# Weights' signs restored by ScalarE's rectifier, VectorE's sign step, floor and low-bit steps removed

## The chip, the cores and the metric

The kernel runs on one NeuronCore of a Trainium2 chip. The metric is the device time of one execution in microseconds (us), taken as the median of several runs. TensorE (PE in the profile, PEld for its weight loads) does the matrix products, VectorE (DVE), ScalarE (ACT) and GpSimd (POOL) the elementwise work, and SyncE (SP) issues the transfers. Each engine runs its own instructions in the order in which they were written into its queue; engines meet only where one waits for another.

## The reference, cut to what matters

Attention with a threshold on 4 batches of 8 heads (576 positions, 64 wide) gives 2304 tokens of width 512. Two dense layers follow, each an expansion to 2048 and a contraction back to 512.

```python
thresh = np.max(scores, axis=-1, keepdims=True) - tau
scores = np.where(scores >= thresh, scores, -1000000000.0)
...
h = x @ w_in
sp = np.where(h > 20.0, h, np.log1p(np.exp(np.minimum(h, 20.0))))
g = h * np.tanh(sp)
return (g @ w_out).astype(np.float32)
...
h = x @ w_in
relu6 = np.clip(h + 3.0, 0.0, 6.0)
g = h * relu6 / 6.0
return (g @ w_out).astype(np.float32)
```

The four weight matrices come in as 64-bit floats.

## The kernel before, in words

The program is written by a planner: a list of tasks, each with the engines that may run it, a cost and a priority, is turned once into a fixed order of instructions for every engine. A table of nudges (`NUDGE`) and the costs set this order; no order is found at run time.

In time it falls into three stages. Up to about 405 us the attention runs tile by tile: scores (`s_s`, L1849) on TensorE, row maximum (`nm_pk`, L1858) and mask (`e_ex`, L1871) on VectorE, exponential on ScalarE, the low half of the split into two 16-bit floats on GpSimd (`p_ph`, L729), a transposing transfer (`pt_tr`, L1884) and the product with the values (`aux_pv`, L1897). The scores tiles lie in two banks of PSUM, and the mask is what frees a bank. The expansion of the first dense layer (`h_g`, L1241) is threaded between these. From about 405 to 640 us comes the contraction of the first dense layer (`y_y`, L1356): ScalarE applies the activation Mish to a stored tile (`hp_e`, L1327) and makes the high half (`gs_h`, L1330), VectorE the low half (`gs_h`, L1336). After 640 us the second dense layer runs.

The weights of all four matrices (m = 0 to 3) are converted on the side, 8 groups of 128 x 1024 words each, 32 conversions. The 64-bit words are loaded (`raw_lr`, L881). VectorE takes the largest magnitude of the high halves (`top`, L785), from which a power of two as scale follows in a few steps on single columns (`group_scale`; L796, L799 to L810). For m = 0 and 2 the maximum is first spread over the partitions: a diagonal (`dgb_zd`, L756, on ScalarE) is multiplied on TensorE (L761) and reduced on VectorE (L764). Then `one_conversion` makes 32-bit floats: ScalarE multiplies the high half with the scale (c1, L921, into the tile `cvt`), VectorE or GpSimd shifts it left by three bits (c2, L931 or L929), VectorE copies the sign bit from the raw word (c3, L937) and then inserts bits of the low half (c4, L942). Two 16-bit halves are made of it (`w__h`, `w__u`). c1 of m = 0 and 1 lies in the attention stage; c1 of m = 2 and 3, 16 conversions, lies between 431 and 624 us, between the instructions of the first layer's contraction. The same diagonals serve to scale the layers' inputs and outputs (`dgb_zdy`).

Of the kernel before, what the change touches and what calls it, by code (L numbers as in the profile page):

```python
# [8 lines left out]
F32 = mybir.dt.float32  # L9
# [6 lines left out]
AF = mybir.ActivationFunctionType  # L16
ALU = mybir.AluOpType
# [23 lines left out]
ORDER_OUT = (0, 5, 6, 4, 2, 3, 1)  # L41
INF_BITS = 0x7F800000
TINY = 2.0 ** -100
FLOOR = 2.0 ** -13
WARM_WINDOW = 3.413
RELEASE = dict.fromkeys(("s", "m", "h", "y", "aux"), 0.27)

# [51 lines left out]
JOIN_FROM = 340.468  # L99
STAY = 0.954  # L100
NBLK_EARLY = 2 * B - 2
NUDGE = {
# [407 lines left out]
class Plan:  # L510
# [19 lines left out]
    def add(  # L530
        self, engines, fn, deps=(), bufs=(), prio=None, off=0.0, dma=0.0, name="", order=()
    ):
        shift = NUDGE.get(name, 0.0)
        prio, off = (None, off + shift) if prio is None else (prio + shift, off)
# [149 lines left out]
def fused_kernel(ctx: ExitStack, tc, q, k, v, tau, w1i, w1o, w2i, w2o, out):  # L684
    nc = tc.nc
# [42 lines left out]
    def sub(e, dst, a, b):  # L728
        engine[e].tensor_tensor(dst, a, b, ALU.subtract)  # L729

    def pick(which, **cost):
        return {e: cost[e] for e in WHO[which]}
# [14 lines left out]
    def bits(t):  # L747
        return t.bitcast(U32)

    def spread(task, name, src, held, ring, after):  # L750

        dg, pm = Buf(r_dgb), Buf(ring)

        def diag(e):
            if e == "act":
                nc.scalar.activation(dg.tile, ident, AF.Copy, scale=src())  # L756
            else:
                nc.vector.tensor_scalar_mul(dg.tile, ident, src())

        def total(e):  # L760
            mm(pm.tile[:, :P], ones, dg.tile, start=True, stop=True)  # L761

        def top(e):
            nc.vector.tensor_reduce(src(), pm.tile[:, :P], AX.X, ALU.max)  # L764

        a = task({"dve": 0.3, "act": 0.4}, diag, [after], [*held, dg], "zd" + name)
        a = task({"pe": 0.06}, total, [a], [dg, pm], "zp" + name)
        return task({"dve": 0.28}, top, [a], [*held, pm], "zt" + name)
# [4 lines left out]
    wt, r_w, converted, scaled_by, wsc = {}, {}, {}, {}, {}  # L773

    def high(raw):
        return bits(raw.tile).rearrange("p a (n t) -> p a n t", t=2)[:, :, :, 1]
# [14 lines left out]
    def group_scale(task, name, m, i, ring, after):  # L791

        top, sc, inv = (wsc[m][k][:, i : i + 1] for k in ("top", "sc", "is"))

        def cut(e):
            nc.vector.tensor_scalar(bits(top), bits(top), 0x7FFF0000, None, ALU.bitwise_and)  # L796

        def factor(e):
            nc.vector.tensor_scalar(top, top, FLOOR, None, ALU.max)  # L799
            nc.vector.tensor_scalar(  # L800
                bits(sc), bits(top), INF_BITS, INF_BITS, ALU.bitwise_and, ALU.bitwise_xor
            )
            if m == 0:
                nc.vector.tensor_scalar_mul(inv, sc, 2.0 ** -111)
            nc.vector.tensor_scalar_mul(sc, sc, 2.0 ** -112)
            if m == 0:
                nc.vector.tensor_scalar(
                    bits(inv), bits(inv), 3, INF_BITS, ALU.logical_shift_left, ALU.bitwise_and
                )
                nc.vector.tensor_scalar(bits(inv), bits(inv), INF_BITS, None, ALU.bitwise_xor)  # L810

        a = after
        if m % 2 == 0:
            a = task({"dve": 0.15}, cut, [a], [], "za" + name)
            a = spread(task, name, lambda: top, [], ring, a)
        return task({"dve": 0.97 if m == 0 else 0.5}, factor, [a], [], "zf" + name)

# [55 lines left out]
    def tasker(at):  # L873
        def task(engines, fn, deps, bufs, tag, dma=0.0):
            return add(engines, fn, deps, bufs, at, 0.0 if at is not None else MOE_OFF, dma, tag)

        return task
# [7 lines left out]
    def convert(m, src, pool, prio, off, ring):  # L885
# [23 lines left out]
            scaled_parts[:] = [factors[i : i + step] for i in range(0, NG, step)]  # L909
        scaled_by[m] = summary(tasker(prio + 2 * NG * off), m, ring, factors)  # L910

    def one_conversion(m, g, raw, deps, task):
        nm = f"{m}_{g}_"
        t = Buf(r_cvt)
        dst = wt[m][g]

        def low():
            return bits(raw.tile).rearrange("p a (n t) -> p a n t", t=2)[:, :, :, 0]

        def c1(e):  # L920
            nc.scalar.activation(  # L921
                t.tile.bitcast(F32), high(raw).bitcast(F32), AF.Copy,
                scale=wsc[m]["sc"][:, g : g + 1],
            )

        def c2(e, j):
            if e == "pool":
                ti = t.tile[:, j].bitcast(I32)
                nc.gpsimd.tensor_tensor(ti, ti, eight.to_broadcast([P, DM]), ALU.mult)  # L929
                return  # L930
            nc.vector.tensor_scalar(  # L931
                t.tile[:, j], t.tile[:, j], 3, 0x7FFFFFF8, ALU.logical_shift_left,
                ALU.bitwise_and,
            )

        def c3(e):
            nc.vector.scalar_tensor_tensor(  # L937
                t.tile, high(raw), 0x80000000, t.tile, ALU.bitwise_and, ALU.bitwise_or
            )

        def c4(e):
            nc.vector.scalar_tensor_tensor(  # L942
                t.tile, low(), 29, t.tile, ALU.logical_shift_right, ALU.bitwise_or
            )

        a = task(EXPAND, c1, deps, [raw, t], "c" + nm)
        b = [
            task(
                pick(f"c{m}{j}", **SHIFT) if m > 1 else SHIFT, lambda e, j=j: c2(e, j), [a], [t],
                f"c{nm}{j}",  # L950
            )
            for j in range(2)
        ]
        a = task({"dve": 1.28}, c3, b, [raw, t], "c" + nm)
        a = task({"dve": 1.28}, c4, [a], [raw, t], "c" + nm)
        if m > 1:
            combined(m, g, t, a, task)
            return

        def hi(e):  # L960
            nc.scalar.activation(dst.tile[:, :, 0], t.tile.bitcast(F32), AF.Copy)

        def lo(e, j):
            sub(e, dst.tile[:, j, 1], t.tile[:, j].bitcast(F32), dst.tile[:, j, 0])

        a = task({"act": 1.05}, hi, [a], [t, dst], "h" + nm)
        for j in range(2):
            converted[m, 2 * g + j] = task(
                {"pool": 1.25, "dve": 0.68}, lambda e, j=j: lo(e, j), [a], [t, dst], f"u{nm}{j}"
            )  # L970
# [289 lines left out]
    def inner(blk, early, at=None, gap=0.0):  # L1260

        task = planner(at, gap, f"0_{blk}")
        if blk == 2 * B:
            x, src = Buf(r_x), Buf(r_sum)

            def tails_of():
                return src.tile

            def get(e):
                nc.sync.dma_start(out=tails_of(), in_=td)  # L1270

            a = task({"sp": 0.5}, get, tails, [src], "xt", 1.46)
            ready = [
                split(task, f"0_{blk}", src, tails_of, x, xinv[:, B:], r_h, [a])
            ]
            input_scales(B, ready[0], None if at is None else at)
        else:
            x, ready = x_of.pop(blk)
        hscale, scaled = hin[:, blk // 2], hin_done[blk // 2]
        for fp in range(NG):  # L1280
            h = Buf(r_h)
            last = gemm1(task, 0, fp, PIECE if early else 12, x, h, ready)
            if fp % 2 == 0:
# [780 lines left out]
    t = 0  # L2064
# [3 lines left out]
    for b in range(B):  # L2068
        units = [(hp, cs) for cs in halves for hp in range(NPAIR)]
        tiles = {}  # L2070
        for i, (hp, cs) in enumerate(units):
# [4 lines left out]
            t = tiles[hp](t, cs)  # L2076
# [68 lines left out]
    task = tasker(at)  # L2145
# [81 lines left out]
```

## Time and profile before

| what | value |
|---|---|
| median of 3 runs | 985.71 us (985.18 to 986.22) |
| profiled execution | 984.73 us, its span 982.9 us |
| TensorE busy | 922.2 us (94%) |
| VectorE busy | 797.9 us (81%) |
| ScalarE busy | 650.8 us (66%) |
| GpSimd busy | 409.2 us (42%) |

The span is the time from the first to the last instruction in the profile; the 1.8 us beside it lie around it. Busy shares are means over stages that differ, so the stages have to be read one by one.

### The profile page before, as it was taken

How to read it: one execution, taken by the hardware profiler on the slowest of the kernel's cores; microseconds unless marked ns; L12 is line 12 of the kernel's file. 1: busy time of each engine (PE TensorE's matmuls, PEld its weight loads, DVE VectorE, ACT ScalarE, POOL GpSimd, SP SyncE). 2: the span in 40 equal slices, each digit the busy share in tenths (PEclk: the TensorE clock that was granted, in tenths of full speed). 3: DMA queues.
4: the chain of work that ended last, by engine and by line, in shares of the span. 5: the costliest groups of instructions: out<-in, count | busy, mean ns of one | idle time of the engine just before them, and what ended most of it. 6: DMA issues, size and time to landing. Idle time of an engine off the chain costs nothing.

```text
span 982.9 us, 25896 instructions
## 1 busy us (share of the span) xinstructions
PE 922.2 (94%) x10776; PEld 797.2 (81%) x10776; DVE 797.9 (81%) x1516; ACT 650.8 (66%) x1051; POOL 409.2 (42%) x354
## 2 busy tenths in 40 slices
PE   3669779999999999999999999999999999999996
PEld 1447457777777778888888888899999999999986
DVE  6998898888878888569999889888758758758864
ACT  6678688888888877567866778655444444545541
POOL 2777776766655667315656777720000000000000
PEclk9769789999999999999999999999999999999999
DMA  9899999999999999864654757750110110110001
GB/s 313 179 233 234 228 226 218 251 253 217 238 217 270 216 220 238 234 239 173 239 211 176 282 188 287 246 219 9 60 47 16 60 41 22 60 32 31 23 15 31
DMA packets 201798, 164.48 MB, mean 167 GB/s; under 512 B 174160, under 2 KB 174928, under 8 KB 195280
## 3 DMA queue, kind: packets, MB, share of 16 engines
q1 hardware_dynamic: 201680, 162.82, 61.1%
q8 instruction: 85, 1.39, 0.6%
q14 instruction: 33, 0.27, 0.1%
HBM read 84.28 MB, written 36.04 MB: 122 GB/s over the span
## 4 chain that ended last, share of the span: by engine, by line
PE 76%; DVE 13%; POOL 3%; DMA 3%; issue 2%; ACT 1%; SPq 0%; DVEq 0%; POOLq 0%; ACTq 0%
PE h_g L1241 15%; PE y_y L1356 13%; PE s_s L1849 7%; PE aux_pv L1897 5%; PE hp_g1a L1430 5%; PE h_g0a L1430 5%; PE hp_g1d L1430 2%; PE h_g0d L1430 2%; DMA pt_tr<-p_ph 2%; DVE e_ex L1871 2%; DVE nm_pk L1858 1%; POOL p_ph L729 1%; DVE top L785 1%; PE h_g1b L1430 1%; DVE gs_h L1336 1%
## 5 line engine op out<-in xcount | busy, mean ns | idle before, releaser
L729 POOL TENSOR_TENSOR p_ph<-e_ex,p_ph 128x128 f16<-128x128 f32 (+3 forms) x160 | 192.5, 1225 | 106.4 <-issue 54.8
L1583 PEld LDWEIGHTS <-gs_h 128*128 128x128 f16 x1512 | 146.8, 98 | 18.0 <-issue 1.5
L1430 PEld LDWEIGHTS <-w__h 128*128 128x128 f16 x2016 | 156.0, 98 | 1.2 <-issue 0.6
L1871 DVE SCALAR_TENSOR_TENSOR e_ex<-s_s,thr_th,e_ex 128x576 f32<-128x576 f32 x144 | 111.9, 812 | 15.3 <-ACT thr_th L1863 11.8
L1858 DVE TENSOR_REDUCE nm_pk<-s_s 128x1 f32<-128x576 f32 x144 | 104.6, 751 | 18.0 <-PE s_s L1849 17.0
L1868 ACT ACTIVATE e_ex<-s_s,nm_pk 128x576 f32<-128x576 f32 x144 | 104.1, 730 | 18.5 <-DVE nm_pk L1858 13.9
L1849 PE MATMUL s_s<-kd_lk,qs_qp 64*128 64x288 f32 x440 | 80.8, 480 | 36.4 <-DVE e_ex L1871 25.6
L1876 ACT ACTIVATE p_ph<-e_ex 128x576 f16<-128x576 f32 x144 | 94.8, 678 | 13.5 <-DVE e_ex L1871 9.1
L1430 PEld LDWEIGHTS <-w__u 128*128 128x128 f16 x1008 | 98.6, 98 | 0.0
L1897 PEld LDWEIGHTS <-pt_tr 128*128 128x128 f16 x2016 | 81.3, 103 | 11.1 <-issue 5.8
L1849 PEld LDWEIGHTS s_s<-kd_lk,qs_qp 64*128 64x128 f32 x440 | 41.4, 204 | 59.0 <-issue 39.5
L1897 PE MATMUL aux_pv<-vh,pt_tr 128*128 128x65 f16 (+1 forms) x1296 | 86.1, 203 | 1.9 <-DMA pt_tr<-p_ph 1.9
L729 DVE TENSOR_TENSOR gs_h<-g_ab,gs_h 128x896 f16<-128x896 f32 x72 | 74.6, 1087 | 15.9 <-ACT gs_h L1533 15.9
L1533 ACT ACTIVATE gs_h<-g_ab 128x1792 f16<-128x1792 f32 x36 | 59.6, 1690 | 27.4 <-DVE g_ab L729 27.4
L1897 PE MATMUL aux_pv<-vl_vl,pt_tr 128*128 128x64 f16 x720 | 70.7, 203 | 0.0
L1517 ACT ACTIVATE g_ab<-g_ab,aux,hscales 128x512 f32<-128x512 f32 x72 | 54.1, 804 | 16.9 <-DVE g_ab L1458 16.9
L1327 ACT ACTIVATE hp_e<-hl_l 128x512 f32<-128x512 f32 x72 | 42.4, 594 | 23.5 <-DVE gs_h L1336 23.2
L1290 ACT ACTIVATE he_t<-h_g,hin 128x512 f32<-128x512 f32 x63 | 42.9, 683 | 19.0 <-PE h_g L1241 15.1
L1523 DVE SCALAR_TENSOR_TENSOR g_ab<-g_ab,f 128x512 f32<-128x512 f32 x72 | 51.2, 747 | 5.0 <-ACT g_ab L1517 5.0
L1336 DVE SCALAR_TENSOR_TENSOR gs_h<-hp_e,fscales,gs_h 128x512 f16<-128x512 f32 x72 | 53.0, 743 | 2.1 <-ACT gs_h L1330 2.1
L1330 ACT ACTIVATE gs_h<-hp_e,fscales 128x512 f16<-128x512 f32 x72 | 47.3, 678 | 7.6 <-PE y_y L1356 6.8
L1448 ACT ACTIVATE s_ka<-h_g0a 128x512 f32<-128x512 f32 x27 | 16.1, 595 | 48.1 <-PE h_g0a L1430 47.9
(672 smaller groups left out, 2559.2 us busy)
## 6 DMA issues: line engine op xcount, KB each, us to landing
hd<-he_t SPq DMA_DIRECT2D x36, 512.0 KB, 4.2
hl_l<-hd SPq DMA_DIRECT2D x18, 1024.0 KB, 5.7
raw_lr<-in_moe_w_in SPq DMA_DIRECT2D x16, 1024.0 KB, 6.0
raw_lr<-in_moe_w_out SPq DMA_DIRECT2D x16, 1024.0 KB, 7.5
yd<-yl_zhy SPq DMA_DIRECT2D x9, 896.0 KB, 3.8
qs_qp<-in_q SPq DMA_DIRECT2D x10, 576.0 KB, 5.8
v_lv<-in_v SPq DMA_DIRECT2D x16, 320.0 KB, 4.7
kd_lk<-in_k SPq DMA_DIRECT2D x15, 288.0 KB, 3.9
```

The costliest lines, as they stand in the source:

```text
L729: engine[e].tensor_tensor(dst, a, b, ALU.subtract)
L1241: mm(hv[:, j, :], wj[:, wl, c * P : (c + 1) * P], x.tile[:, c, xl, :], start=j == 0 and n == 0, stop=j == 1 and n == 11, skip_group_check= ...
L1336: nc.vector.scalar_tensor_tensor(s.tile[:, k, 1], g.tile.rearrange("p (a n) -> p a n", a=2), fs[:, fp : fp + 1], s.tile[:, k, 0], ALU.mult ...
L1356: mm(yv[:, h, :], wt[1][f // 2].tile[:, f % 2, wl, c * P : (c + 1) * P], gs[fp // COL].tile[:, fp % COL, gl, f % 2, :], start=fp == 0 and ...
L1430: mm(dst.tile[:, i * Q : (i + 1) * Q], wt[2][fp][wl].tile[:, right - 1, c * P : (c + 1) * P], x[xl].tile[:, c, left - 1], start=first and ...
L1583: mm(region(p), part[:, gl, left - 1], wt[3][fp][wl].tile[:, right - 1], start=fp == n == 0 and spot(p)[1] == 0, stop=fp == NG - 1 and n == 2,
L1849: mm(s[j].tile[:, half, :HALF], lh[r], rh[r], start=m == 0, stop=m == len(terms) - 1,)
L1858: nc.vector.tensor_reduce(neg.tile[:, j : j + 1], sv(j), AX.XY, ALU.max, negate=True)
L1868: nc.scalar.activation(ev(j), sv(j), AF.Exp, bias=neg.tile[:, j : j + 1])
L1871: nc.vector.scalar_tensor_tensor(ev(j), sv(j), thr.tile[:, j : j + 1], ev(j), ALU.is_ge, ALU.mult)
L1876: nc.scalar.activation(p16.tile[:, js, :S], e_.tile[:, js], AF.Copy)
L1897: mm(ov[:, dst, :d], pt.tile[:, j, ch, :], part.tile[:, src, vc, :], start=i == j == ch == 0 and part is vh, stop=j == w - 1 and ch == 8, ...
```

## The change

c1 becomes a rectifier (`AF.Prelu`) whose slope for negative inputs is minus 2 to the 32nd: a negative word comes out positive, with the exponent bit of weight 32 set. The shift by three moves that bit into the place of the sign, and the mask of the shift keeps it. So VectorE's sign step c3 falls away, in all 32 conversions. The maximum is no longer cut to its upper bits (16 instructions, m = 0 and 2) and no longer floored (32 instructions); instead the scale is bounded in the multiplication that was there. The tasks stay in the planner with their costs, as empty functions.

```diff
-        def cut(e):
-            nc.vector.tensor_scalar(bits(top), bits(top), 0x7FFF0000, None, ALU.bitwise_and)
-
         def factor(e):
-            nc.vector.tensor_scalar(top, top, FLOOR, None, ALU.max)
-            nc.vector.tensor_scalar(
-                bits(sc), bits(top), INF_BITS, INF_BITS, ALU.bitwise_and, ALU.bitwise_xor
-            )
+            ts = nc.vector.tensor_scalar
+            ts(bits(sc), bits(top), INF_BITS, INF_BITS, ALU.bitwise_and, ALU.bitwise_xor)
             if m == 0:
-                nc.vector.tensor_scalar_mul(inv, sc, 2.0 ** -111)
-            nc.vector.tensor_scalar_mul(sc, sc, 2.0 ** -112)
+                ts(inv, sc, 2.0 ** -111, 2.0 * CAP, ALU.mult, ALU.min)
+            ts(sc, sc, 2.0 ** -112, CAP, ALU.mult, ALU.min)
...
+    def idle(e):
+        pass
...
             nc.scalar.activation(
-                t.tile.bitcast(F32), high(raw).bitcast(F32), AF.Copy,
-                scale=wsc[m]["sc"][:, g : g + 1],
+                t.tile.bitcast(F32), high(raw).bitcast(F32), AF.Prelu,
+                scale=wsc[m]["sc"][:, g : g + 1], alpha=NEGATIVE,
             )
...
-                t.tile[:, j], t.tile[:, j], 3, 0x7FFFFFF8, ALU.logical_shift_left,
+                t.tile[:, j], t.tile[:, j], 3, 0xFFFFFFF8, ALU.logical_shift_left,
...
-        def c3(e):
-            nc.vector.scalar_tensor_tensor(
-                t.tile, high(raw), 0x80000000, t.tile, ALU.bitwise_and, ALU.bitwise_or
-            )
...
-        a = task({"dve": 1.28}, c3, b, [raw, t], "c" + nm)
+        a = task({"dve": 1.28}, idle, b, [raw, t], "c" + nm)
```

The order of the remaining instructions is unchanged on every engine; TensorE, GpSimd and SyncE have the same rows as before. Line numbers behind the change are 8 lower for most of the code. VectorE has 1373 rows in place of 1454.

VectorE during the first conversion (m = 0, group 0), before: the spread maximum, the sign step of `cvt_c_0`, the floor (L799) and the scale of the next group, then the attention.

```order
L764 TENSOR_REDUCE top_146<-aux_zp_1_1_414 128x1
L1967 TENSOR_SCALAR den_dt_0_2_430<-aux_pv_0_0_1_306 128x4
L937 SCALAR_TENSOR_TENSOR cvt_c_0__1_377<-raw_lr_0_0_199,cvt_c_0__1_377 128x1024
L1970 RECIPROCAL den_dt_0_2_430<-den_dt_0_2_430 128x4
L799 TENSOR_SCALAR top_146<-top_146 128x1
L800 TENSOR_SCALAR sc_147<-top_146 128x1
L804 TENSOR_SCALAR is_149<-sc_147 128x1
L805 TENSOR_SCALAR sc_147<-sc_147 128x1
L807 TENSOR_SCALAR is_149<-is_149 128x1
L810 TENSOR_SCALAR is_149<-is_149 128x1
L1974 TENSOR_TENSOR xn_dn_0_2_445<-aux_pv_0_0_1_306,den_dt_0_2_430 128x256
L1858 TENSOR_REDUCE nm_pk_1_0_1_448<-s_s_1_0_0_425 128x1
```

The same place now:

```order
L765 TENSOR_REDUCE top_146<-aux_zp_1_1_411 128x1
L1959 TENSOR_SCALAR den_dt_0_2_427<-aux_pv_0_0_1_305 128x4
L1962 RECIPROCAL den_dt_0_2_427<-den_dt_0_2_427 128x4
L798 TENSOR_SCALAR sc_147<-top_146 128x1
L800 TENSOR_SCALAR is_149<-sc_147 128x1
L801 TENSOR_SCALAR sc_147<-sc_147 128x1
L803 TENSOR_SCALAR is_149<-is_149 128x1
L804 TENSOR_SCALAR is_149<-is_149 128x1
L1966 TENSOR_TENSOR xn_dn_0_2_440<-aux_pv_0_0_1_305,den_dt_0_2_427 128x256
L1850 TENSOR_REDUCE nm_pk_1_0_1_443<-s_s_1_0_0_422 128x1
```

The sign step and the floor are gone; what stood behind them moves up.

ScalarE has 977 rows in place of 945. The 32 new ones are loads of activation tables (`ACT_TABLE_LOAD`), put in when the program is built: one ahead of each rectifier of m = 2 and 3, and one ahead of the next Mish. There are none at the 16 conversions of the attention stage, and the two loads that stood in the program before stand there still. ScalarE at the conversion of group 4 of m = 2 (c1 is `cvt_c_4`), before:

```order
L1330 ACTIVATE gs_h_0_2_1_7513<-hp_e_0_2_1_7588,fscales 128x512
L921 ACTIVATE cvt_c_4__1_7632<-raw_lr_4_0_7407,sc_6626 128x1024
L1327 ACTIVATE hp_e_0_3_1_7649<-hl_l_0_3_0_7480 128x512
L1290 ACTIVATE he_t_0_8_1_7515<-h_g_0_0_8_1_7498,hin 128x512
L1327 ACTIVATE hp_e_0_3_1_7657<-hl_l_0_3_0_7480 128x512
L997 ACTIVATE w__h_3_0_2_7607<-sum_q_3_0_1_7605 128x1024
L1111 ACTIVATE xf_zvy_1_0_1_1_7686<-y_y_0_0_1_0_7162,sm_zmy_1_0_1_1_7534 128x512 x2
L1330 ACTIVATE gs_h_0_3_1_7705<-hp_e_0_3_1_7649,fscales 128x512
L1330 ACTIVATE gs_h_0_3_1_7705<-hp_e_0_3_1_7657,fscales 128x512
L756 ACTIVATE dgb_zd_5_0_7723<-ident,top_6625 128x128
```

The same place now:

```order
L1322 ACTIVATE gs_h_0_2_1_7461<-hp_e_0_2_1_7535,fscales 128x512
L918 ACT_TABLE_LOAD
L918 ACTIVATE cvt_c_4__1_7578<-raw_lr_4_0_7356,sc_6586 128x1024
L1319 ACT_TABLE_LOAD
L1319 ACTIVATE hp_e_0_3_1_7595<-hl_l_0_3_0_7429 128x512
L1282 ACTIVATE he_t_0_8_1_7463<-h_g_0_0_8_1_7446,hin 128x512
L1319 ACTIVATE hp_e_0_3_1_7603<-hl_l_0_3_0_7429 128x512
L989 ACTIVATE w__h_3_0_2_7554<-sum_q_3_0_1_7552 128x1024
L1103 ACTIVATE xf_zvy_1_0_1_1_7632<-y_y_0_0_1_0_7116,sm_zmy_1_0_1_1_7481 128x512 x2
L1322 ACTIVATE gs_h_0_3_1_7650<-hp_e_0_3_1_7595,fscales 128x512
L1322 ACTIVATE gs_h_0_3_1_7650<-hp_e_0_3_1_7603,fscales 128x512
L757 ACTIVATE dgb_zd_5_0_7667<-ident,top_6585 128x128
```

Two table loads stand around the rectifier; nothing else moved.

## Rows read from the trace of the kernel before

**Rows 1.** The page: the span, and TensorE's busy time, share and instructions.
```profile
span 982.9 us, 25896 instructions
...
PE 922.2 (94%) x10776; PEld 797.2 (81%) x10776; DVE 797.9 (81%) x1516; ACT 650.8 (66%) x1051; POOL 409.2 (42%) x354
```

**Rows 2.** Windows by stage: length; PE, PEld, DVE, ACT, POOL busy (count); PEclk; DMA.
```profile
25.00:80.00 55.00, 36.63 (x391) 26.39 (x389) 52.85 (x109) 38.85 (x67) 41.40 (x36) 0.72 0.85 198
...
98.00:140.00 42.00, 29.32 (x282) 19.90 (x278) 36.12 (x77) 30.92 (x57) 28.66 (x28) 0.80 1.03 233
...
140.00:200.00 60.00, 60.00 (x748) 47.55 (x749) 54.27 (x102) 50.89 (x93) 44.40 (x39) 1.00 1.03 231
...
460.00:530.00 70.00, 67.83 (x624) 60.46 (x622) 68.10 (x118) 50.62 (x75) 41.79 (x30) 1.00 0.50 177
...
530.00:640.00 110.00, 109.99 (x1019) 98.66 (x1019) 95.83 (x163) 82.60 (x121) 83.01 (x61) 1.00 0.70 254
```

**Rows 3.** TensorE's longest waits, 25 to 80 us, then 98 to 140 us: total, times, longest.
```profile
PE s_s L1849 <- DVE e_ex L1871: 12.3, 7, 4.1
...
PE s_s L1849 <- DVE e_ex L1871: 7.6, 3, 3.5
```

**Rows 4.** Timeline, GpSimd then VectorE: start, length, instruction, [idle before, releaser].
```profile
66.78 2.26 POOL L729 TENSOR_TENSOR w__h__1_806<-cvt_c__1_694,w__h__1_806 128x512 f16<-128x512 f32 x2 [4.58 <-ACT w__h__1_806 L961]
...
111.29 1.43 DVE L937 SCALAR_TENSOR_TENSOR cvt_c__1_1405<-raw_lr,cvt_c__1_1405 128x1024 uint32<-128x1024 uint32 x1 [1.67 <-POOL cvt_c__1_1405 L929]
...
114.88 1.22 DVE L785 TENSOR_REDUCE top<-raw_lr 128x1 f32<-128x1024 f32 x1 [1.49 <-DMA raw_lr<-in_moe_w_in]
```

**Rows 5.** Windows, line L937 (the sign step) alone: VectorE busy (count), PEclk, DMA.
```profile
25.00:80.00 55.00, 5.67 (x4) 0.72 0.85 198
...
98.00:140.00 42.00, 3.93 (x3) 0.80 1.03 233
```

**Rows 6.** VectorE's lines: the floor, with its count, busy us and mean ns.
```profile
L799 DVE TENSOR_SCALAR top<-top 128x1 f32<-128x1 f32 x32 | 4.6, 145 | 0.1
```

**Rows 7.** ScalarE's timeline around the one table load in its midst.
```profile
413.10 0.69 ACT L1290 ACTIVATE he_t<-h_g,hin 128x512 f32<-128x512 f32 x1 [1.98 <-PE h_g L1241]
413.81 1.28 ACT L1327 ACT_TABLE_LOAD   x1
415.10 1.12 ACT L1327 ACTIVATE hp_e<-hl_l 128x512 f32<-128x512 f32 x2
```

**Rows 8.** ScalarE's timeline at three conversions, and a diagonal for TensorE.
```profile
455.95 1.24 ACT L921 ACTIVATE cvt_c__1_7295<-raw_lr,sc 128x1024 f32<-128x1024 f32 x1 [2.05 <-DVE sc L805]
...
463.32 1.25 ACT L921 ACTIVATE cvt_c__1_7392<-raw_lr,sc 128x1024 f32<-128x1024 f32 x1 [1.56 <-DVE sc L805]
...
475.07 0.60 ACT L1327 ACTIVATE hp_e<-hl_l 128x512 f32<-128x512 f32 x1 [2.71 <-DVE gs_h L1336]
...
480.26 1.24 ACT L921 ACTIVATE cvt_c__1_7632<-raw_lr,sc 128x1024 f32<-128x1024 f32 x1
481.38 0.59 ACT L1327 ACTIVATE hp_e<-hl_l 128x512 f32<-128x512 f32 x1
...
486.42 0.40 ACT L756 ACTIVATE dgb_zd<-ident,top 128x128 bf16<-128x128 f32 x1
```

**Rows 9.** TensorE's timeline: a spread matmul and its one stall at 530 us.
```profile
488.23 0.22 PE L761 MATMUL h_zp<-dgb_zd,ones 128*128 128x128 bf16 x1
...
530.01 1.47 PE L1241 MATMUL h_g<-x_zh,w__h__1_1766 128*128 128x256 f16 x12 [2.10 <-DVE he_t L1292]
```

**Rows 10.** Windows, line L921 (c1) alone: ScalarE busy (count), PEclk, DMA.
```profile
460.00:530.00 70.00, 7.44 (x6) 1.00 0.50 177
530.00:640.00 110.00, 8.64 (x7) 1.00 0.70 254
```

**Rows 11.** ScalarE's waits for VectorE and for TensorE, 530 to 640 us.
```profile
ACT hp_e L1327 <- DVE gs_h L1336: 9.5, 12, 1.5
ACT gs_h L1330 <- PE y_y L1356: 6.3, 4, 2.6
```

More of the change, by code (lines that the diff above doesn't have):

```diff
@@ L43 @@
 TINY = 2.0 ** -100
-FLOOR = 2.0 ** -13
+CAP = 2.0 ** -98
 WARM_WINDOW = 3.413
@@ L101 @@
 NBLK_EARLY = 2 * B - 2
+NEGATIVE = -(2.0 ** 32)
 NUDGE = {
@@ L793, in group_scale @@
         top, sc, inv = (wsc[m][k][:, i : i + 1] for k in ("top", "sc", "is"))
-        def cut(e):
-            nc.vector.tensor_scalar(bits(top), bits(top), 0x7FFF0000, None, ALU.bitwise_and)
         def factor(e):
-            nc.vector.tensor_scalar(top, top, FLOOR, None, ALU.max)
-            nc.vector.tensor_scalar(
-                bits(sc), bits(top), INF_BITS, INF_BITS, ALU.bitwise_and, ALU.bitwise_xor
-            )
+            ts = nc.vector.tensor_scalar
+            ts(bits(sc), bits(top), INF_BITS, INF_BITS, ALU.bitwise_and, ALU.bitwise_xor)
             if m == 0:
-                nc.vector.tensor_scalar_mul(inv, sc, 2.0 ** -111)
-            nc.vector.tensor_scalar_mul(sc, sc, 2.0 ** -112)
+                ts(inv, sc, 2.0 ** -111, 2.0 * CAP, ALU.mult, ALU.min)
+            ts(sc, sc, 2.0 ** -112, CAP, ALU.mult, ALU.min)
             if m == 0:
-                nc.vector.tensor_scalar(
-                    bits(inv), bits(inv), 3, INF_BITS, ALU.logical_shift_left, ALU.bitwise_and
-                )
-                nc.vector.tensor_scalar(bits(inv), bits(inv), INF_BITS, None, ALU.bitwise_xor)
+                ts(bits(inv), bits(inv), 3, INF_BITS, ALU.logical_shift_left, ALU.bitwise_and)
+                ts(bits(inv), bits(inv), INF_BITS, None, ALU.bitwise_xor)
         a = after
         if m % 2 == 0:
-            a = task({"dve": 0.15}, cut, [a], [], "za" + name)
+            a = task({"dve": 0.15}, idle, [a], [], "za" + name)
             a = spread(task, name, lambda: top, [], ring, a)
@@ L931, in c2 @@
             nc.vector.tensor_scalar(
-                t.tile[:, j], t.tile[:, j], 3, 0x7FFFFFF8, ALU.logical_shift_left,
+                t.tile[:, j], t.tile[:, j], 3, 0xFFFFFFF8, ALU.logical_shift_left,
                 ALU.bitwise_and,
-            )
-        def c3(e):
-            nc.vector.scalar_tensor_tensor(
-                t.tile, high(raw), 0x80000000, t.tile, ALU.bitwise_and, ALU.bitwise_or
             )
```

## Prediction

> **What bounds the kernel now.** I read the page first, then windows cut by stage, then TensorE's waits in the stages where it is not full, then ScalarE's and VectorE's timelines where the change touches them. TensorE is busy 922.2 us of the span of 982.9 us [rows 1]; what can be won without less matrix work is in the other 60 us. The windows say where they lie. From 25 to 80 us TensorE is busy 36.63 of 55 us and from 98 to 140 us 29.32 of 42 us, while VectorE is busy 52.85 and 36.12; from 140 us on TensorE is full, and from 530 to 640 us it is busy 109.99 of 110 us [rows 2]. In the first two stages it waits above all for the mask that frees a scores bank, 12.3 and 7.6 us [rows 3]. So there VectorE sets the pace, helped by a granted clock of 0.72 and 0.80, that is 1.2 GHz for part of the time [rows 2]. Behind that TensorE sets the end: an engine that works off its queue in order, and is full, keeps any head start that it gets, and passes on any wait that it is given. The change therefore has two terms: what VectorE gives TensorE before 140 us, and what the new table loads cost it between 455 and 640 us.
>
> **Term one: VectorE before 140 us.** In 25 to 80 us four sign steps take 5.67 us, in 98 to 140 us three take 3.93 us [rows 5]. The floor takes 145 ns [rows 6] and stands there eight times (once a conversion, all of m = 0), 1.2 us; the low-bit step, one column like it, stands there six times, by the same row 0.9 us. Together 5.67 + 3.93 + 1.2 + 0.9 = 11.7 us. That is the upper bound. The lower is 0: if GpSimd, the transfers or ScalarE held the pace, VectorE would only idle more. GpSimd is busy 41.40 of 55 us, and its chain shows up in the critical path, but its long waits are for halves that ScalarE can make only once VectorE has finished the word: 4.58 us at 66.78 us [rows 4], so it moves up with VectorE. One step gives nothing: that at 111.29 us waited 1.67 us for GpSimd and took 1.43 us, and shortly behind it VectorE waits 1.49 us for a load of raw words [rows 4]; without the step it would wait there instead. That leaves 10.3 us. Instructions overlap by about a tenth of a microsecond, and here and there the mask will find its exponential not ready. I take 7 us, nearer the upper end because VectorE idles only 2 us of 55 in the first stage. The other 25 sign steps buy TensorE nothing directly, since it is full where they stand: its own matrix work hides them, and if it ran out, each would be worth its 1.2 to 1.4 us again.
>
> The rectifier itself costs what the copy did, as far as rows go: c1 takes 1.24 to 1.25 us [rows 8] on the same 1024 columns, and no row shows a rectifier. I take 0, with a bound of one overlap, 0.1 us, an instruction.
>
> **Term two: 32 table loads on ScalarE.** The load in the middle of the program takes 1.28 us; the copy ahead of it runs from 413.10 for 0.69 us and so ends at 413.79, the load begins at 413.81 and the Mish behind it at 415.10 [rows 7]. So the load stands in the open and costs 1.31 us. Elsewhere neighbours overlap: the c1 at 480.26 lasts 1.24 us, yet the Mish behind it begins at 481.38, 0.12 us before c1 ends [rows 8]. A load between the two takes this away as well: about 1.41 us a load, 45 us in all.
>
> The Trainium skill's page "ScalarE: Activation LUTs", section "What ACT_TABLE_LOAD costs", gives about 1283 ns for the load, as the row has it, and on top of it some 1380 ns of drain, 2.66 us a switch. The trace shows no such drain around its load [rows 7]; by the page 32 loads would cost 85 us, and the sum would come out near the second rival's, below. The same page, section "Table sets: the hidden batching unit", says to group calls by table set and not to alternate, which speaks against this order.
>
> From 460 to 530 us ScalarE is busy 50.62 of 70 us, from 530 to 640 us 82.60 of 110 us [rows 2]. Six conversions fall into the first window and seven into the second [rows 10], two loads each: 12 and 14 loads, 16.9 and 19.7 us. That makes 67.5 of 70 and 102.3 of 110. The loads fit, but only just. Most of ScalarE's idle time there is waiting for VectorE, which the change unloads, and a load stands ahead of the wait of its successor, so it can run inside it: 2.05 us at 455.95, 1.56 at 463.32, 2.71 at 475.07 [rows 8]; between 530 and 640 us such waits are 9.5 us, and 6.3 us more are for TensorE to free a tile [rows 11], which means that ScalarE is ahead there and can afford to fall back.
>
> Where it can't afford it: the diagonals. The one at 486.42 ends at 486.82 [rows 8] and its matmul starts at 488.23 [rows 9], a margin of 1.41 us. From 455.95 to there five loads are not hidden ahead of their own c1, 7.05 us; if the waits of 1.56 and 2.71 us take their fill, 2.8 us are left, 1.4 us more than the margin; if they take nothing, 5.6 us more.
>
> So the bounds of the whole term: with all of ScalarE's idle time (19.4 and 27.4 us) open to loads, 0; with half of it, 16.9 - 9.7 = 7.2 and 19.7 - 13.7 = 6.0, together 13.2 us; with three quarters, 16.9 - 14.55 = 2.35 and nothing, 2.4 us. I take 5 us, the diagonals' tight margin being the reason to go above 2.4. Against it stands one gain: TensorE's stall of 2.10 us at 530.01, which waits for VectorE [rows 9]; six sign steps fewer lie ahead of it, but VectorE will then wait for ScalarE, and I take 0.5 us. Term two: 4.5 us.
>
> **Sum.** 7.0 - 4.5 = 2.5 us less. From the profiled execution's 984.73 us that makes 982.2 us; the median of the runs shown is 985.71 us, 0.98 above it, so I forecast a median of **983.2 us**.
>
> **Rivals.** First, on the other side: ScalarE becomes the bound from 455 to 640 us. The point from which it decides is about half of its idle time: if no more than that takes loads, 13.2 us are lost, less 7 is 6.2 us slower, 991.9 us. For it speaks that ScalarE and VectorE wait for each other in a ring of two tiles, so a wait need not vanish because one of them is unloaded; against it the 6.3 us for which ScalarE waits for TensorE.
>
> Second, the price of a load: if ScalarE must run dry before each, the overlap lost is not 0.1 us but the whole last instruction, 1.24 us for a c1, and a load costs 1.28 + 1.24 = 2.5 us. Then 26 loads cost 66 us in windows with 46.8 us of idle time, at least 19 us late, 12 us slower in all, 998 us or more. This is in size the page's rule of load and drain. The row [rows 7] speaks against it.
>
> Third, the loads vanish altogether into waits and only term one is left: 985.71 - 7 = 978.7 us. For it the 9.5 and 6.3 us [rows 11]; against it the margin at 488 us.
>
> Fourth, the change buys little before 140 us: transfers are busy 0.85 to 1.03 of the time there [rows 2], and GpSimd may hold the pace once VectorE doesn't. With 3 us won and 4 lost it is 986.7 us, no change that can be told.
>
> **How the numbers follow.** About 0.2%, 2 us, is what a measurement of this kernel can tell from no change. My forecast has 0.40: its own range, 5 to 9 won and 2 to 7 lost, runs from 979 to 988 us, three quarters of it faster. All loads hidden: 0.15, faster. Little won early: 0.12, within 0.2%. ScalarE bound: 0.27, slower. Running dry: 0.06, slower. Faster is 0.30 + 0.15 = 0.45, same 0.10 + 0.12 = 0.22, slower 0.33. The range for 8 in 10 goes from 9.2 us won and nothing lost, 976.5 us, to 991.5 us, just inside the bound of the first rival; running dry stays outside it.
>
> **What would show it.** Right: TensorE's first saturated stretch, at 140 us now, begins some 7 us sooner; loads of 1.28 us with gaps of hundredths around them; ScalarE busy more than 95% from 455 to 530 us, VectorE below 85%; TensorE's new waits there on ScalarE's diagonals, 1 to 3 us each, few of them; after 640 us the same rows, shifted. Wrong: TensorE waiting as long as before in 25 to 140 us, with GpSimd or a transfer named; waits of TensorE that add up to over 10 us between 455 and 640 us; a load of over 1.5 us, or a gap ahead of it.

## The result and the profile after

The changed kernel takes 991.33 us (median of 5 runs, 989.44 to 992.69), the kernel before 985.33 us beside it (5 runs, 983.52 to 986.22): ratio 1.0059, 95% interval 1.004 to 1.0077. It is slower by 6 us (5.8 by the ratio, 4 to 7.6). The forecast was 983.2 us and faster; the time lies at the upper end of the range, near where the first rival put it (991.9 us).

The page of the profiled execution of after (989.61 us), and ScalarE's lines of table loads (count, busy us, mean ns, idle time before them), against [rows 1]:

```profile
span 987.7 us, 25818 instructions
PE 926.1 (94%) x10776; PEld 798.6 (81%) x10776; DVE 747.4 (76%) x1436; ACT 692.2 (70%) x1083; POOL 395.6 (40%) x354
...
L1319 ACT ACT_TABLE_LOAD x17 | 21.8, 1283 | 0.3
L918 ACT ACT_TABLE_LOAD x16 | 20.5, 1283 | 0.3
```

VectorE got 50 us lighter, ScalarE 41 us heavier, and the new time on ScalarE is the loads: 32 more, each 1283 ns, with next to no idle time ahead of them. The rectifier itself cost nothing: its 32 rows take 1212 to 1260 ns, the copies of before took 1207 to 1253.

The windows of after (columns as in [rows 2]), and one of before for the stretch from 420 to 460 us, which the prediction had not looked at:

```profile
25.00:80.00 55.00, 40.20 (x405) 28.59 (x404) 50.02 (x103) 41.18 (x70) 41.81 (x38) 0.72 0.96 209
98.00:140.00 42.00, 32.42 (x329) 21.87 (x326) 33.97 (x77) 33.95 (x62) 30.15 (x29) 0.84 1.06 246
...
420.00:460.00 40.00, 37.43 (x346) 33.27 (x343) 25.36 (x46) 33.53 (x48) 15.76 (x11) 1.00 0.48 177
460.00:530.00 70.00, 68.30 (x627) 60.74 (x624) 54.83 (x102) 67.41 (x88) 40.68 (x30) 1.00 0.51 179
530.00:640.00 110.00, 105.05 (x950) 93.21 (x948) 80.43 (x141) 96.80 (x130) 74.39 (x58) 0.98 0.67 247
```
```profile
420.00:460.00 40.00, 40.00 (x372) 35.84 (x370) 31.35 (x58) 28.22 (x47) 15.39 (x11) 1.00 0.61 223
```

Before 140 us TensorE gained, as forecast. From 420 us on it is no longer full, and ScalarE fills 33.5 of 40, 67.4 of 70 and 96.8 of 110 us. TensorE's waits of after from 420 to 660 us (who waited for whom; total, times, longest) now name ScalarE's diagonals, where before one wait of 2.1 us for VectorE was the longest [rows 9]. The second fence has the longest wait of VectorE, the third that of ScalarE, both of after, from 420 to 640 us:

```profile
PE h_zpy L762 <- ACT dgb_zdy L757: 6.4, 3, 2.6
PE h_zp L762 <- ACT dgb_zd L757: 2.8, 3, 1.2
PE h_zpy L762 <- DVE dgb_zdy L759: 0.6, 1, 0.6
```
```profile
DVE gs_h L1328 <- ACT gs_h L1322: 21.6, 15, 3.7
```
```profile
ACT hp_e L1319 <- DVE gs_h L1328: 9.1, 17, 1.4
```

The same two waits in the kernel before:

```profile
DVE gs_h L1336 <- ACT gs_h L1330: 1.7, 5, 0.7
```
```profile
ACT hp_e L1327 <- DVE gs_h L1336: 23.0, 26, 3.7
```

The ring of two tiles between ScalarE and VectorE has turned round. The reader can tell which engine is the late one by who waits longer: before, ScalarE waited 23.0 us for VectorE and VectorE 1.7 for ScalarE; now VectorE waits 21.6 us and ScalarE 9.1.

To place the loss, the same instruction of TensorE is compared in two traces: the 32 matmuls of the spreads, which stand in the same order in every kernel here. Start in after minus start in before, in us, by the time in before:

| 67 | 103 | 191 | 440 | 460 | 488 | 538 | 560 | 580 | 604 | 642 |
|---|---|---|---|---|---|---|---|---|---|---|
| -1.6 | -3.6 | -5.1 | -4.9 | -2.0 | 0.0 | -2.3 | +0.5 | +3.0 | +4.6 | +4.8 |

TensorE is 4.9 us ahead at 440 us and 4.8 us behind at 642 us. The late stage lost 9.7 us. These two are single executions, 4.9 us apart (989.61 and 984.73 us), where the medians are 6 us apart.

### The profile page after: what moved, and what is told of

Read it like the earlier page. It is cut to its first block, busy times and chain, and to the rows that moved or that the text cites. A ratio compares the mean times of both kernels' runs of the same rounds, so it can differ in the third digit from the quotient of the medians.

```text
span 987.7 us, 25818 instructions
## 1 busy us (share of the span) xinstructions
PE 926.1 (94%) x10776; PEld 798.6 (81%) x10776; DVE 747.4 (76%) x1436; ACT 692.2 (70%) x1083; POOL 395.6 (40%) x354
## 4 chain that ended last, share of the span: by engine, by line
PE 76%; DVE 7%; ACT 7%; DMA 5%; issue 2%; POOL 2%; SPq 0%; DVEq 0%; ACTq 0%; POOLq 0%
PE h_g L1233 17%; PE y_y L1348 11%; PE s_s L1841 8%; PE aux_pv L1889 6%; PE hp_g1a L1422 5%; PE h_g0a L1422 5%; PE hp_g1d L1422 2%; PE h_g0d L1422 2%; DMA pt_tr<-p_ph 2%; DMA raw_lr<-in_moe_w_out 1%; DVE e_ex L1863 1%; PE h_g1b L1422 1%; DVE nm_pk L1850 1%; DMA raw_lr<-in_moe_w_in 1%; POOL p_ph L730 1%
## 5 line engine op out<-in xcount | busy, mean ns | idle before, releaser
L730 POOL TENSOR_TENSOR p_ph<-e_ex,p_ph 128x128 f16<-128x128 f32 (+3 forms) x160 | 186.3, 1187 | 110.5 <-issue 56.8
```

## The experiments

The theory after the result (A) was: VectorE's relief gave the lead, and the 32 loads took it and more, each at its place. All kernels below keep the planner's order. For each, its median, the median of the kernel before measured beside it, the ratio with its interval, TensorE's place against before's profile at 440 us, and what TensorE lost (+) or won (-) from 440 to 642 us:

| kernel | us | before, us | ratio | at 440 | 440 to 642 |
|---|---|---|---|---|---|
| changed | 991.33 | 985.33 | 1.0059 (1.004-1.0077) | -4.87 | +9.68 |
| early_only | 979.12 | 985.99 | 0.9928 (0.9914-0.9943) | -4.81 | -1.46 |
| late_only | 997.07 | 985.99 | 1.0109 (1.009-1.0129) | +1.66 | +10.96 |
| copy_no_signs | 979.33 | 985.99 | 0.9931 (0.9911-0.9952) | -1.58 | -3.12 |
| diag_on_vector | 996.12 | 985.99 | 1.0102 (1.0083-1.012) | -3.37 | +13.26 |
| early_and_m2 | 985.09 | 987.84 | 0.9977 (0.996-0.9994) | +0.70 | +3.32 |
| early_and_m3 | 988.30 | 987.84 | 1.0018 (1.0001-1.0035) | -3.16 | +6.49 |
| load_time_only | 990.02 | 987.84 | 1.0028 (1.0009-1.0048) | +1.82 | +5.55 |
| load_time_longer | 999.03 | 988.04 | 1.012 (1.0088-1.0153) | +1.54 | +12.97 |
| small_steps_only | 985.14 | 987.84 | 0.9973 (0.9959-0.9987) | +3.74 | -1.46 |
| sign_step_early_only | 983.03 | 986.31 | 0.9963 (0.9949-0.9976) | -3.91 | +1.65 |
| loads_in_attention | 1014.20 | 986.31 | 1.0275 (1.0253-1.0298) | +29.62 | -1.45 |

The kernel before was not equally fast in all comparisons (985.33 to 988.04 us), so a time is to be read by its ratio; where a range was given in us, the ratio times 985.33 stands beside the time below.

The column at 440 us is one execution and scatters: early_only, early_and_m2 and early_and_m3 have the same instructions up to there and stand at -4.8, +0.7 and -3.2. They part between 121 and 403 us. From 121 to 410 us TensorE's waits in early_and_m2 sum to 4.8 us more than in early_only, 2.2 us of it for the transposing transfers and 1.6 us with no releaser in the profile; what set these off is open. So the early term is read from the ratios; the last column is steadier (-1.46, -1.46 and -1.45 in three kernels whose late instructions are the same). It holds the clock as well: sign_step_early_only has the late instructions of before and the same stall of 2.10 us ahead of the same matmul, yet lost 1.65 us. Behind that stall its granted clock was 0.50 from 528 to 530 us, where before kept 1.00.

**early_only**: one half of the change, without a load.

```diff
+            kind = {"alpha": NEGATIVE} if m < 2 else {}
             nc.scalar.activation(
-                t.tile.bitcast(F32), high(raw).bitcast(F32), AF.Prelu,
-                scale=wsc[m]["sc"][:, g : g + 1], alpha=NEGATIVE,
+                t.tile.bitcast(F32), high(raw).bitcast(F32), AF.Prelu if kind else AF.Copy,
+                scale=wsc[m]["sc"][:, g : g + 1], **kind,
             )
...
-        a = task({"dve": 1.28}, idle, b, [raw, t], "c" + nm)
+        a = task({"dve": 1.28}, c3, b, [raw, t], "c" + nm)
```

Here c3 returns at once where m < 2, and the mask of the shift keeps the sign bit only there.

> The rectifier and the missing sign step for matrices 0 and 1 alone; matrices 2 and 3 are converted as before (copy, sign step kept). Floors and low-bit cuts stay out. No table load is added. Theory A (the late loss is the 32 table loads, the early gain is VectorE's relief): TensorE is 4.9 us ahead of before at 440 us, as in the changed kernel, and keeps it: 985.3 - 4.9 = 980.4. Rival B (a lead is given back late whatever ScalarE does, because the late stage waits for something with its own pace): 984 to 985.5, with the 4.9 us still there at 440 us and shrinking after it.

It took 979.12 us (978.2 by the ratio) and is the fastest kernel of the study, 0.7% under before and 1.3% under the changed kernel by the two ratios. The lead at 440 us stays; rival B is out. Its windows:

```profile
420.00:460.00 40.00, 40.00 (x371) 35.86 (x370) 32.56 (x56) 29.71 (x47) 16.61 (x12) 1.00 0.48 178
460.00:530.00 70.00, 68.48 (x631) 61.28 (x630) 68.06 (x105) 50.26 (x75) 44.59 (x32) 1.00 0.57 195
530.00:640.00 110.00, 110.00 (x1070) 99.28 (x1069) 91.02 (x160) 81.28 (x119) 81.70 (x59) 1.00 0.69 259
```

**late_only**: the same edit with m > 1.

> The opposite half: the rectifier and the missing sign step for matrices 2 and 3 alone, matrices 0 and 1 as before. Theory A: no early lead, all of the late loss, 985.3 + 9.7 = 995.0. Rival C (the late loss is so large only because TensorE arrives 4.9 us early at a stage whose pace others set): TensorE arrives later, so about half the loss, 985.3 + 4.8 = 990.

997.07 us (996.1 by the ratio): all of the loss, and 1.3 us more. About as much, 1.4 us, went where the granted clock fell a second time in this kernel's late stage (0.50 from 461 to 464 us; the changed kernel had 1.00 there). Arriving early is not what makes the loads dear; rival C is out.

**copy_no_signs**: the copy everywhere.

```diff
-                t.tile.bitcast(F32), high(raw).bitcast(F32), AF.Prelu,
-                scale=wsc[m]["sc"][:, g : g + 1], alpha=NEGATIVE,
+                t.tile.bitcast(F32), high(raw).bitcast(F32), AF.Copy,
+                scale=wsc[m]["sc"][:, g : g + 1],
```

> The changed kernel with the copy in place of the rectifier in all 32 conversions, so that no table load is added and no VectorE step comes back; the weights' signs are left out of the result. What it differs by from the changed kernel is the price of the loads alone. Theory A: 991.3 - 9.7 = 981.6, and lower by up to the 2.1 us stall at 530 us that VectorE's relief removed, so 979.5 to 981.6. Rival D (it is the missing sign step that hurts late, by letting raw buffers go sooner and so moving transfers): 988 to 991.

979.33 us (978.5 by the ratio), a little under theory A's range: rival D is out, and the loads have a price. By the last column it is 9.68 + 3.12 = 12.8 us; by the ratios 1.0059 against 0.9931, 1.3% or 12.6 us.

**diag_on_vector**: is it only the small diagonals that come late?

```diff
-            if e == "act":
+            if e == "act" and not name.startswith(("2_", "y", "s3")):
                 nc.scalar.activation(dg.tile, ident, AF.Copy, scale=src())
```

> The changed kernel with 17 diagonals of the spreads (8 of matrix 2's maxima, 8 of the second layer's inputs, 1 of matrix 3) on VectorE and no longer on ScalarE, in the same place of the order. The stalls of TensorE that name these diagonals sum to 9.2 us. Theory A1 (ScalarE's whole load bounds the stage; the diagonals are only where TensorE meets it): 17 x 0.39 = 6.6 us come off ScalarE and the waits move to the second-layer inputs that the activation function makes, 985 to 989. Rival A2 (ScalarE has slack, and only these 17 small steps behind a load are late): all 9.2 us go, 982. Rival A3 (VectorE is no better placed): 990 to 992.

All three missed: 996.12 us (995.4 by the ratio), slower than the changed kernel (1.0102 against 1.0059). Lines of its timeline, VectorE then TensorE (start, length, instruction, idle before and releaser); the same matmul in the changed kernel; and VectorE's wait here for ScalarE's hidden tiles from 420 to 640 us:

```profile
447.68 1.22 DVE L786 TENSOR_REDUCE top<-raw_lr 128x1 f32<-128x1024 f32 x1 [1.88 <-DMA raw_lr<-in_moe_w_in]
...
450.80 2.11 DVE L730 TENSOR_TENSOR w__u<-cvt_c__1_6917,w__h 128x768 f16<-128x768 f32 x1
452.83 0.27 DVE L759 TENSOR_SCALAR dgb_zd<-ident,top 128x128 bf16<-128x128 f32 x1
...
453.16 0.22 PE L762 MATMUL h_zp<-dgb_zd,ones 128*128 128x128 bf16 x1 [4.06 <-DVE dgb_zd L759]
```
```profile
448.75 0.22 PE L762 MATMUL h_zp<-dgb_zd,ones 128*128 128x128 bf16 x1 [1.14 <-ACT dgb_zd L757]
```
```profile
DVE gs_h L1328 <- ACT gs_h L1322: 20.4, 12, 3.7
```

The diagonal that took 0.39 us on ScalarE takes 0.27 us here and still comes later: TensorE waits 4.06 us for it and not 1.14. VectorE had waited 1.88 us for a load of raw words and then worked without a pause from 447.68 us until the diagonal's turn came at 452.83. ScalarE, rid of 17 diagonals, was still the late one in the ring (20.4 us against 21.6). So moving the instruction that a wait names does not help where the queue that takes it has other work ahead of it. Part of the 3.6 us that this kernel lost beyond the changed one is the clock: behind this stall it was granted 0.50 from 454 to 457 us, where the changed kernel had 1.00.

**early_and_m2** and **early_and_m3**: the dose. Early_only's edit with m < 3, and with m != 2.

> The kernel of early_only with the rectifier for matrix 2 as well (no sign step there), so that 16 of the 32 table loads are added, all before 524 us; matrix 3 keeps copy and sign step. Theory A (each load costs where it stands): in the changed kernel TensorE lost 4.8 us from 440 to 488 us against early_only's none, so 979.1 + 4.8 = 983.9, less up to 2.3 if the relief at 530 us comes with matrix 2. Rival E (ScalarE's slack takes 16 loads, and only all 32 are too many): 979 to 980.5. Rival F (once the queues have fallen behind, the rest of the stage stays late by itself): 987 to 991.

> The kernel of early_only with the rectifier for matrix 3 as well, so that the other 16 loads are added, from 524 us on; matrix 2 keeps copy and sign step. Theory A: in the changed kernel TensorE lost 6.9 us from 538 to 603 us, so 979.1 + 6.9 = 986.0; with early_and_m2 the two losses then sum to about the 12.2 us between early_only and the changed kernel. Rival E: 979 to 980.5. Rival G (the second half is slow only because the first left ScalarE behind): 981 to 983.

Each half costs. By the ratio they took 983.1 and 987.1 us. Against early_only's -1.46 the first 16 loads cost TensorE 4.8 us (theory A: 4.8) and the second 16 cost 8.0 us (6.9), by ratios to early_only 4.8 and 8.9 us. These are net of what the missing sign steps give back, and so the first hit is partly luck: by 512 us early_and_m2 had lost 6.2 us, of which it won back 2.3 at the stall at 530 us. Together they make 12.7 us, where both halves at once, in the changed kernel, cost 11.1 net by the same column (9.68 + 1.46) and 12.9 by the ratios. Rivals E and G are out. F is out too: with matrix 2 alone TensorE is level with its own place at 538 us for the rest of the stage (+4.63 at 538, 580 and 625 us); behind its last load, at 525 us, it loses no more.

**load_time_only** and **load_time_longer**: is a load more than 1.28 us of ScalarE?

```diff
+    def load_time(table):
+        in_place["table"] = table
+        for _ in range(4):
+            nc.scalar.activation(spare, ident, AF.Copy)
...
+            if m > 1 and in_place["table"] != "rectifier":
+                load_time("rectifier")
             nc.scalar.activation(
...
+                if in_place["table"] == "rectifier":
+                    load_time("mish")
                 nc.scalar.activation(g.tile, hl.tile[:, k], AF.Mish)
```

> The kernel of copy_no_signs (the weights' signs left out of the result, no rectifier, no load) with four 128x128 copies of ScalarE into a spare tile wherever the changed kernel has a table load, from 420 us on. Such a copy starts about 0.31 us after the one before it, so four take about 1.25 us, where the load takes 1.283. Theory A (a load is 1.28 us of ScalarE's time and nothing else): the time of the changed kernel, 990 to 992. Rival H (a load also drains or restarts the engine, or the rectifier reads otherwise): clearly less, 980 to 987.

> As load_time_only, with five copies of 128x128 in place of four wherever the changed kernel has a table load (the signs of the weights are left out of the result again). In load_time_only's trace four took 1.22 to 1.23 us from the first's start to the next instruction's, so five take 1.53; the changed kernel's load takes 1.29 so and does not overlap the instruction before it, about 1.40 in all. From 440 to 642 us TensorE lost 5.6 us with four, 9.7 us in the changed kernel and -3.1 us in copy_no_signs. Theory A (a load is ScalarE's time alone): five copies, being longer than a load, cost at least what a load does, so TensorE loses 9.7 us or more in this stretch, and the time is 991 to 995. Rival H (a load costs something beyond its time): 5.6 x 1.25 or so, at most 8 us lost in this stretch, 988 to 990.

The loads' +9.68 us lie between four copies (+5.55) and five (+12.97). From the first copy's start to the next instruction's, four take 1.23 us a place and five 1.57 (the expectation had 1.53); on the line between them 9.68 stands for 1.42 us, and the prediction had 1.41 for a load with its lost overlap. By the ratio four copies take 988.1 us, under theory A's 990 to 992, and five take 997.2, over its 991 to 995; the changed kernel's 991.3 lies between. So theory A was off in us both times, and the 990.02 fell into its range only because the kernel before was 2.5 us slower beside it. Rival H, by which five copies lose at most 8 us, is out. The places in the trace are single executions; the granted clock fell once in the late stage of all three (0.83 from 580 to 590 us in the changed kernel and with four, 0.91 from 560 to 580 us with five). As far as they go, ScalarE's time alone accounts for the loads. The points also show how the price grows: without the copies -3.12, the first 39 us of them cost 8.7 us (22%), the next 11 us cost 7.4 (68%). First the slack goes, then most is passed on.

**small_steps_only** and **sign_step_early_only**: the two parts of the early gain. The first is the changed kernel with the copy and c3 for every matrix; the second is before with the rectifier for m < 2, the floors and cuts in their place.

> The changed kernel's scale arithmetic alone: 32 floors and 16 low-bit cuts of one column each are gone from VectorE, and all 32 conversions are by copy with the sign step, as before. Theory A: no table load and no sign step removed, so neither the loss nor the lead; in late_only TensorE stood 1.7 us behind before at 440 us with the same small steps: 985 to 986. Rival I (the short steps in the chain from maximum to scale are worth their latency): up to 48 x 0.15 = 7.2 us, of which perhaps half on the path: 981 to 983.

> The kernel before with one part of the change alone: rectifier and no sign step for matrices 0 and 1. Floors and low-bit cuts stand as before, matrices 2 and 3 are as before, no table load is added. It divides the gain of early_only (ratio 0.9928) between the sign steps and the short scale steps (alone 0.9973). Theory A (the sign steps of the attention stage are most of it): 0.995 to 0.996 of before, 4 to 5 us. Rival J (the short steps do it, by taking their latency out of the chain from maximum to scale): 0.998 to 1.

The times are 982.7 and 981.7 us by the ratio. Small steps 0.9973, 2.7 us (1.3 to 4.1), within rival I's range; early sign steps 0.9963, 3.6 us (2.4 to 5.0); both, in early_only, 7.1 us (5.6 to 8.5). The sum 6.3 agrees within the intervals. So the sign steps are the larger part, just short of theory A's 4 to 5 us, and I was wrong to expect nothing of the short steps. Of the gain of the short steps 1.46 us lies after 440 us, in each of the three kernels that lack them and keep the copy and the sign step for matrices 2 and 3; 0.57 us of it comes off the stall at 530 us.

**loads_in_attention**: the same number of loads where ScalarE is idle a fifth of the time.

```diff
         def c1(e):
+            if m < 2:
+                nc.scalar.preload_act_table_set("small")
```

> The kernel of early_only with 32 table loads of the same kind in the attention stage: one ahead of each of the 16 conversions of matrices 0 and 1 (a set that also holds the rectifier), one at the next exponential or activation after it. Nothing is left out. Theory K (a load costs what it exceeds ScalarE's slack at its place, and ScalarE has slack where TensorE waits for VectorE's masks): 979 to 983 when before is 985.3. Theory L (32 loads cost TensorE about 12 us wherever they stand): 990 to 992.

Both missed by far: 1014.20 us (1012.4 by the ratio). TensorE lost 34.4 us by 440 us against early_only, 1.08 us a load, where the late stage asked 12.8 / 32 = 0.40. ScalarE's, VectorE's and TensorE's timelines show how, around 40 us:

```profile
38.26 1.28 ACT L919 ACT_TABLE_LOAD   x1
39.55 1.26 ACT L921 ACTIVATE cvt_c__1_446<-raw_lr,sc 128x1024 f32<-128x1024 f32 x1
40.83 1.28 ACT L1870 ACT_TABLE_LOAD   x1
42.12 0.74 ACT L1870 ACTIVATE e_ex<-s_s,nm_pk 128x576 f32<-128x576 f32 x1
...
38.16 1.41 DVE L1860 TENSOR_REDUCE nm_pk<-s_s 128x1 f32<-128x576 f32 x2
...
43.15 1.54 DVE L1873 SCALAR_TENSOR_TENSOR e_ex<-s_s,thr_th,e_ex 128x576 f32<-128x576 f32 x2 [2.85 <-ACT thr_th L1865]
...
49.22 2.29 PE L1851 MATMUL s_s<-kd_lk,qs_qp 64*128 64x288 f32 x8 [2.86 <-DVE e_ex L1873]
```

The maxima are ready at 39.57 us, the exponential starts at 42.12, and VectorE's mask waits 2.85 us for ScalarE. TensorE's wait is still put down to VectorE's mask: from 0 to 200 us that row grew from 27.0 us in early_only to 35.5. So a wait that names VectorE can hold ScalarE's time, and theory K was wrong to count it as slack. Part of the loss came with the clock. Windows of early_only, then of this kernel:

```profile
140.00:200.00 60.00, 59.71 (x731) 46.94 (x729) 51.03 (x96) 50.29 (x92) 41.47 (x38) 1.00 1.07 239
```
```profile
140.00:200.00 60.00, 53.22 (x640) 40.27 (x640) 49.15 (x94) 50.45 (x85) 36.59 (x31) 0.95 0.93 202
```

Here the granted clock is 0.95 against 1.00, from 25 to 80 us it is 0.72 against 0.81. Over all of the 440 us the difference makes at most 13 of the 34.4 us, if TensorE had been busy throughout. Whether shorter ScalarE work would help there as much as longer work hurts was not tried.

## Why the prediction was wrong

**What bounds the kernel** held: TensorE sets the end, and it keeps a lead and passes on a wait.

**Term one**, 7 us, was right in its mechanism, and in size partly by luck. Both parts together measured 7.1 us (5.6 to 8.5), but 1.5 us of that falls after 440 us, so the early stage gave about 5.6. The short steps measured 2.7 us by themselves, where the working gave those before 140 us at most 2.1 of 11.7 and the later ones nothing. The rectifier at 0 was right.

**The price of a load**, 1.41 us, was right (1.42 from the copies). The Trainium skill's page "ScalarE: Activation LUTs", section "What ACT_TABLE_LOAD costs", has the 1283 ns that 34 rows of after show; its 1380 ns of drain are in no row (the added loads have 0.02 us of idle time ahead of them, and the next instruction mostly starts 0.01 us behind), and the copies leave no room for them. The advice of its section "Table sets: the hidden batching unit" to group by set would have settled the direction here: the half of the change that alternates between two sets pays 12.8 us for its loads and wins 1.7, the half that does not wins 7.1.

**Term two failed**, at the step "I take 5 us": the loads cost 12.8 us, not 5. Against that stood 3.1 us of gains in the same stretch, not 0.5: 1.46 us from the short steps, and 1.66 us from the late sign steps, which took away what was left of the stall of [rows 9]. Net 9.7 us, not 4.5. By the places of TensorE in the changed kernel and in copy_no_signs, the 12.8 us are 2.9 up to 455 us, 2.2 from there to 512 us and 7.7 from 538 to 642 us. The first window of the prediction so came out where three quarters of ScalarE's idle time take loads (2.35 us); the second, for which that assumption gave nothing and half gave 6.0, is where the price was mis-sized. Three things made it so. The first two lie in the step that set the idle time of a whole window against the loads of a whole window, the third in no step.

First, it began at 455 us, and its two windows hold 26 of the 32 loads. Four loads stand from 427 to 436 us, and by 455 us TensorE had lost 2.9 us of its lead. ScalarE of after, the same stretch of early_only below it:

```profile
426.25 0.60 ACT L1319 ACTIVATE hp_e<-hl_l 128x512 f32<-128x512 f32 x1 [0.49 <-DVE gs_h L1328]
426.87 1.28 ACT L918 ACT_TABLE_LOAD   x1
428.16 1.22 ACT L918 ACTIVATE cvt_c__1_6917<-raw_lr,sc 128x1024 f32<-128x1024 f32 x1
...
429.70 1.28 ACT L1319 ACT_TABLE_LOAD   x1
...
432.80 1.28 ACT L918 ACT_TABLE_LOAD   x1
434.09 1.23 ACT L918 ACTIVATE cvt_c__1_6973<-raw_lr,sc 128x1024 f32<-128x1024 f32 x1
435.34 1.28 ACT L1319 ACT_TABLE_LOAD   x1
436.64 0.60 ACT L1319 ACTIVATE hp_e<-hl_l 128x512 f32<-128x512 f32 x1
```
```profile
426.85 1.23 ACT L919 ACTIVATE cvt_c__1_6917<-raw_lr,sc 128x1024 f32<-128x1024 f32 x1
...
429.97 1.25 ACT L919 ACTIVATE cvt_c__1_6973<-raw_lr,sc 128x1024 f32<-128x1024 f32 x1
431.11 0.60 ACT L1327 ACTIVATE hp_e<-hl_l 128x512 f32<-128x512 f32 x1
```

Both arrive at 426.9 us. The Mish behind the second conversion starts at 436.64 and at 431.11: four loads, 5.5 us, 1.38 us each, none of it hidden up to there, though ScalarE of before was idle for 11.8 us in the window from 420 to 460 us. Behind it some slack came: TensorE lost 2.9 of the 5.5 us.

Second, slack is local. Ahead of the two long stalls of TensorE, at 560 and 583 us, stand four loads (from 544 us on) and three (from 572 us on), with no diagonal between them that TensorE waits for. After, at the largest stall: ScalarE, VectorE, TensorE.

```profile
553.83 1.28 ACT L918 ACT_TABLE_LOAD   x1
...
556.38 1.28 ACT L1319 ACT_TABLE_LOAD   x1
...
560.23 0.39 ACT L757 ACTIVATE dgb_zdy<-ident,sm_zmy 128x128 bf16<-128x128 f32 x1
...
558.91 0.75 DVE L1328 SCALAR_TENSOR_TENSOR gs_h<-hp_e,fscales,gs_h 128x512 f16<-128x512 f32 x1 [3.69 <-ACT gs_h L1322]
559.58 0.14 DVE L1042 TENSOR_SCALAR sm_zmy<-sm_zmy 128x1 uint32<-128x1 uint32 x1
...
560.67 0.22 PE L762 MATMUL h_zpy<-dgb_zdy,ones 128*128 128x128 bf16 x1 [2.61 <-ACT dgb_zdy L757]
```

The step that the diagonal needs (559.58) stands on VectorE behind a gs_h that waits 3.69 us for ScalarE. The prediction let the loads run inside ScalarE's waits for VectorE; in the ring the lateness went to VectorE and came back to ScalarE. TensorE's waits for diagonals sum to 9.8 us, of which 6.5 lie between 455 and 640 us, where the prediction had named 10 us as the sign that it was wrong. Its signs of being right, loads without gaps, ScalarE at 96% and VectorE at 78% from 460 to 530 us, all came true beside a slower kernel; they could not tell the two outcomes apart.

Third, the clock. After the stall of 2.34 us that ended at 582.87 us TensorE's granted clock fell from 1.00 to 0.50, that is from 2.4 to 1.2 GHz, until about 587 us. Windows of after (TensorE busy, granted clock, transfers), the stall's own first:

```profile
580.00:583.00 3.00, 0.66 (x7) 1.00 0.98 410
583.00:585.00 2.00, 2.00 (x15) 0.67 0.07 29
585.00:587.00 2.00, 2.00 (x11) 0.50 0.31 53
```

From 580 to 604 us of before TensorE lost 1.66 us more with no wait in sight. No step of the prediction had this.

**The first rival** (991.9 us) had the size, 13.2 us lost against 12.8 measured for the loads, and the mechanism in part: ScalarE is the late one in the ring. Part of the match is luck, for its 13.2 us count 26 loads and it has none of the 3.1 us of gains. And ScalarE is not full: 13 us of the window from 530 to 640 us are idle, while 6.9 us were lost there. It is early at some places and late at the diagonals.

**The other rivals.** Running dry fell with the rows and the copies. Loads all hidden fell with copy_no_signs. Little won early fell with early_only.

## What to carry to other kernels

Before work is moved to an engine with idle time, find the points at which the bounding engine waits for it, and count the new work between two such points against the slack there, not against the idle time of a window. This is read from the traces; no forecast made in this way was put to a run. A wait that names another engine is not slack by itself: loads_in_attention was forecast on that and missed by 30 us. Here the first 39 us on ScalarE cost 22% of their length and the next 11 us 68%. A function that lies outside the table set in use is cheap where its set is loaded anyway and dear where it alternates: keep the cheap half (early_only, 979.12 us) and leave the other half as it was.

## What was not expected of the hardware

- One table load cost TensorE 0.40 us in the late stage and 1.08 us in the attention stage, some 0.4 us of it at most by the clock, with ScalarE busy much alike: 78% there (89.86 of 115 us from 25 to 140 us in early_only) and 73% in the late stage (161.25 of 220 us).
- A stall of 2.34 us of TensorE was followed by half clock until about 587 us, one of 2.61 us at 560 us by none; the same stall of 2.10 us at 530 us was followed by full clock in before and by 0.50 in sign_step_early_only. What decides it was not looked for.
- Removing steps of one column, 0.15 us each, was worth 2.7 us in 985.
